# Two last differences on VectorE, later landings in the planner, and every place worked out anew in a fused attention and highway kernel

## The chip, the cores and the metric

The kernel runs on one core of a Trainium2 chip. The metric is the time of one execution on the device, in microseconds. Five engines of the core run side by side, each through its own instructions in order: TensorE (PE, with its weight loads as PEld), VectorE (DVE), ScalarE (ACT), GpSimd (POOL) and SyncE (SP). Transfers are carried by 16 DMA engines; the load queue is filled by GpSimd instructions, the store queue by SyncE, and one store by ScalarE.

## The reference

Four batches of q, k and v, each 6336 x 256 in f32. A 256 x 256 attention between channels is applied to v; the result goes row by row through a highway layer.

```python
qn = q / (np.linalg.norm(q, axis=1, keepdims=True) + 1e-06)
kn = k / (np.linalg.norm(k, axis=1, keepdims=True) + 1e-06)
s = kn.transpose(0, 2, 1) @ qn / tau
a = softmax(s)                       # over the last axis
x = (v @ a)                          # all batches: 25344 rows of 256
H = np.maximum(x @ w_h, 0.0)
T = 1.0 / (1.0 + np.exp(-(x @ w_t + b_t)))
return T * H + (1.0 - T) * x
```

## The kernel before

**Tiling.** A batch's 6336 rows are 49 slices of 128 rows and a remainder of 64. Loads bring groups of slices (QG for q and k, VG for v) and cast them to f16; q, k and v have rings of 4, 4 and 3 group buffers. A load is a GpSimd instruction, and it waits until the group that last used its buffer has been read.

**Scores.** For each slice S(b, j), TensorE adds k^T q into a 256 x 256 sum (L205, two matmuls of 256 columns) and the Gram matrix of k (L208, two of 128 columns), whose diagonal gives the norms of k. The norms of q come in one of two ways: two more matmuls of 128 columns (L214), or, for a run of four slices, squares on ScalarE (L398), a sum of halves on GpSimd (L404) and a reduction on VectorE (L411), after which the four slices need no L214. `decide` starts a run where a group has four slices left from a multiple of four and fewer than SQ_LATE runs are under way.

**The chain.** When a batch's scores are complete, `make_chain` works a chain of short steps: norms (junk, L449), square roots (ScalarE for batch 0, the GpSimd power L475 for the others), inverses and the diagonal dcat (L494, VectorE), cq on TensorE (L503), logits (L508), exponentials on ScalarE with a table load on either side (L519, L435), the normalised matrix mr (L533), its transposition at (L544), the copies at_sb (L555), the product ah with both weight matrices (L563), and its copies (L574). Then mr holds three 256 x 256 matrices, one for x, one for H and one for the gate.

**Slots.** The output is made in 100 slots of two slices (25 for each batch, the last of each with the remainder, called the odd pair). Slot t transposes v (T, L236, TensorE into PSUM), copies it to SBUF (C, L250, VectorE or ScalarE), and multiplies it by mr three times: Z into zbank, H into h, X into x (L260, four matmuls of 256 columns each). ScalarE takes the sigmoid tt of Z (L301) and seeds the bank anew with the bias (L304). VectorE makes th = max(h, 0) tt (L309) and ux = (tt - 1) x (L317). The output th - ux is a subtraction (L335) on GpSimd, except that the last DVE_SUBS slots have theirs on VectorE. Four slots make one store; the last four slots are stored singly, the very last from ScalarE's queue. LASTS puts the odd pair of the last batch at place 20 of 25.

**The order.** No scheduler of the compiler places anything. The program itself steps through a simulated time: each piece of work is a `Task` with an assumed length and a list of what it comes after, and each engine has a function (`step_pe`, `step_act`, `step_dve`, `step_pool`, `step_sp`) that picks, at each instant, the next task of its lists that is ready. The order in which tasks were picked is the order of the instructions on that engine, fixed for good; on the chip each instruction waits for what it needs. A load is assumed to land when a modelled queue has moved it, and a task that needs it may start 0.15 us later. `slot_of_score` gives the slot at which a score slice is due (from S_END), and scores of the next batch may be taken up to four slots early when TensorE has nothing else. The list `order` sorts the loads by due place. Scores of batch b + 1 are made during the slots of batch b, batch 0's scores alone at the start. A store is held while the DMA queues are full unless ORING - 3 groups of output are ready.

Of instruction names in the text: S, T, C, Z, H, X with a number are those tasks of a slice or slot, k1.0 is group 0 of batch 1 of k.

Of the kernel before, what the change touches and what calls it, by code (L numbers as in the profile page):

```python
# [60 lines left out]
def kernel(  # L61
# [13 lines left out]
    B, N, C = q.shape  # L75
# [4 lines left out]
    NS = N // P  # L80
# [3 lines left out]
    NPAIR = (NS + 1) // 2  # L84
    NSLOT = B * NPAIR
# [7 lines left out]
        return got  # L93

    QG = [spans(4, 8, 8, 8, 8, 8, 3, 2), spans(4, 4, 12, 12, 12, 5)]
    QG += [spans(4, 12, 12, 12, 9)] * (B - 2)
    VG = [spans(8, 8, 8, 12, 13)] + [spans(12, 12, 12, 13)] * (B - 1)
    GT = {"q": 12, "k": 12, "v": 13}
    CH = 4
    SQR, SQ_LATE = 4, 2  # L100
    CLOSE = 44
    DVE_SUBS, ACT_COPIES = 1, 77
    QRING, VRING, ORING = 4, 3, 7
    TTR, THR, VTR = 4, 4, 6
    OG = 4
    LASTS = list(range(20)) + [NPAIR - 1] + list(range(20, NPAIR - 1))
    PAIRS = [list(range(NPAIR))] * (B - 1) + [LASTS]
    S_END = [18, 43, 68]

    ctx.enter_context(tc.manual_schedule())  # L110
    const_pool = ctx.enter_context(tc.tile_pool(name="consts", bufs=1))
# [21 lines left out]
    MM = lambda n: n / 2400.0 + 0.0025  # L133
    PE_LAG, LAG, TO_PE = 0.20, 0.08, 0.10
    TILE = 0.309
    STEP = 0.01

# [244 lines left out]
    def make_run(b, g, j):  # L384
        n = len(runs)
        first = n == 0 or runs[-1].name[1] != b
        half = 1 if first else 2

        def area(m):
            if m % SQR == len(areas):  # L390
                areas.append(
                    work_pool.tile([P, CH + 1, C], f32, tag=f"sq{m}", bufs=1, name=f"sq{m}")
                )
            return areas[m % SQR]

        def square(e):
            o = j - QG[b][g][0]
            nc.scalar.activation(  # L398
                out=area(n)[:, 1:, :], in_=tiles["q", b, g][:, o : o + CH, :], func=Act.Square
            )  # L400

        def halves(e):
            sq = area(n)
            nc.gpsimd.tensor_tensor(  # L404
                out=sq[:, 1 : 1 + half, :], in0=sq[:, 1 : 1 + half, :],
                in1=sq[:, 1 + CH - half : 1 + CH, :], op=AluOp.add,
            )

        def reduce(e):
            lo = 1 if first else 0  # L410
            nc.vector.tensor_reduce(  # L411
                out=area(n + 1)[:, 0, :],
                in_=area(n)[:, lo : 1 + CH - half, :].rearrange("p s c -> p c s"),
                axis=mybir.AxisListType.X, op=AluOp.add,
            )

        sq = Task(("sq", b, j), "ACT", 0.2 + CH * C / 1200.0, square)
        ad = Task(("add", b, j), "POOL", 0.1 + half * C * 0.00235, halves, [(sq, LAG)])
        rd = Task(("red", b, j), "DVE", 1.0, reduce, [(ad, LAG)])
        sq.after.append((task_of_load["q", b, g], 0.15))  # L420
        if n >= SQR:
            sq.after.append((runs[n - SQR], LAG))
        if n >= 1:
            rd.after.append((runs[n - 1], LAG))
        runs.append(rd)
        if ("q", b, g) in recycler:
            recycler["q", b, g].after.append((sq, LAG + 0.2))
        queues["ACT.sq"].append(sq)
        queues["POOL.add"].append(ad)
        queues["DVE.red"].append(rd)  # L430
# [203 lines left out]
    for g in range(len(QG[0])):  # L634
        order += [(-100 + g, "q", 0, g), (-100 + g, "k", 0, g)]
    order += [(-94.5, "remq", 0, 0), (-94.5, "remk", 0, 0)]
    order += [(-80, "q", 1, 0), (-80, "k", 1, 0), (-79, "q", 1, 1), (-79, "k", 1, 1)]
    order += [(-78, "w", 0, 0), (-78, "w", 0, 1)]
    order += [(-70, "v", 0, 0), (-69, "remv", 0, 0), (2, "remq", 0, 1), (2, "remk", 0, 1)]

# [4 lines left out]
    for b in range(1, B):  # L645
        for g in range(len(QG[b])):
            if b == 1 and g < 2:
                continue
            at = slot_of_score(b, QG[b][g][0]) - 1.0
            order += [(at, "q", b, g), (at, "k", b, g)]  # L650
    for b in range(B):
        for g in range(len(VG[b])):
            if (b, g) == (0, 0):
                continue
            order.append((b * NPAIR + VG[b][g][0] // 2 - 4, "v", b, g))
    order.sort(key=lambda x: x[0])


# [106 lines left out]
    for kind, e in (("q", "DVE"), ("k", "ACT")):  # L765
        d = Task((kind, 0, 0), "DMA", 0, None)
        task_of_load[kind, 0, 0] = d
        d.end = 6.2


    chains = {}
# [49 lines left out]
    for at, kind, b, g in order:  # L821
        if kind.startswith("rem"):
            units = (2.5 if kind == "remv" else (0.7, 1.8)[g])
            add_load((kind, 0, g), units, lambda e, kk=kind[3:], g=g: load_rem(kk, g))
            continue
        if kind == "w":
            add_load((kind, 0, g), 2.0, lambda e, g=g: load_w(g))
            for ic in range(2):
                chains[0]["ah", ic].after.append((task_of_load[kind, 0, g], 0.15))
            continue  # L830
        if (b, g) == (0, 0) and kind != "v":
            continue
        after = []
        ring = groups[kind]
        size = VRING if kind == "v" else QRING
        if len(ring) >= size:
            pb, pg = ring[-size]
            gs = (VG if kind == "v" else QG)[pb]
            lastj = gs[pg][0] + gs[pg][1] - 1
            if kind == "v":  # L840
                after.append((TR[slot_of[pb, lastj // 2]], PE_LAG + 0.2))
            else:
                after.append((score[pb, lastj], PE_LAG + 0.2))
        ring.append((b, g))
        gs = (VG if kind == "v" else QG)[b]
        add_load((kind, b, g), gs[g][1], lambda e, a=(kind, b, g): load(*a), after)
        if len(ring) > size:
            recycler[(kind,) + ring[-size - 1]] = loads[-1][0]

    for b in range(B):  # L850
        for j in range(NS + 1):
            for kind in "qk":
                d = task_of_load["rem" + kind, 0, min(b, 1)] if j == NS else \
                    task_of_load[kind, b, group_of(QG[b], j)]
                score[b, j].after.append((d, 0.15))
        for i in range(NPAIR):
            for u in range(2):
                s = 2 * i + u
                d = task_of_load["remv", 0, 0] if s == NS else \
                    task_of_load["v", b, group_of(VG[b], s)]  # L860
                TR[slot_of[b, i]].after.append((d, 0.15))

# [27 lines left out]
    def take(n, engine, now, length=None):  # L892
        task = head(n)
        if not can(task, now):
            return False
        if n == "PE.S":
            decide(*task.name[1:], now)
            if task.name[1:] in squares:
                task.length -= 2 * MM(P)
        ptr[n] += 1  # L900
        run(task, engine, now, length)
        return True

    def soon(engine, now, length):
        task = head(engine + ".chain")
        if task is None or task.name[1] not in (0, B - 1):
            return False
        if any(t.end is None for t, _ in task.after):
            return False
        return max(t.end + lag for t, lag in task.after) < now + length  # L910

    slot_now = lambda: ptr["PE.out"] // 3
    PACE = [0.0]

    def step_pe(now):
        if take("PE.chain", "PE", now):
            return True
        t = slot_now()
        s = head("PE.S")
        look = ptr["PE.T"] - t  # L920
        if s is not None:
            _, b, j = s.name
            if b == 0 or slot_of_score(b, j) <= t:
                if take("PE.S", "PE", now):
                    return True
        if look < (2 if t < NSLOT - 6 else 3) and take("PE.T", "PE", now):
            return True
        if take("PE.out", "PE", now):
            return True
        if take("PE.T", "PE", now):  # L930
            return True
        if s is not None and s.name[1] > 0:
            if slot_of_score(*s.name[1:]) <= t + 4 and take("PE.S", "PE", now):
                return True
        return False

    def step_act(now):
        for n in ("ACT.chain", "ACT.tt", "ACT.seed"):
            if take(n, "ACT", now):
                return True  # L940
        ahead = 3 if slot_now() >= ACT_COPIES and ptr["copy"] % 2 == 0 else 1
        wait = slot_now() == 0 and soon("ACT", now, 0.58)
        if not wait and ptr["copy"] - slot_now() < ahead and take("copy", "ACT", now, 0.58):
            return True
# [2 lines left out]
    def step_dve(now):  # L947
        if take("DVE.chain", "DVE", now):
            return True
        if slot_now() == 0 and soon("DVE", now, 0.42):  # L950
            return False
        ahead = 1 if slot_now() >= ACT_COPIES and ptr["copy"] % 2 == 0 else 3
        if ptr["copy"] - slot_now() < ahead and take("copy", "DVE", now, 0.42):
            return True
        if take("DVE.thux", "DVE", now) or take("DVE.sub", "DVE", now):
# [30 lines left out]
    def step_sp(now):  # L986
# [8 lines left out]
        late = nload[0] == len(loads)  # L995
        if dma.backlog(1) > 6.0:
            return False
        if dma.backlog(0) + dma.backlog(1) > 3.0 and ready_groups < ORING - 3 and not late:
            return False
        behind = None  # L1000
        if now > s.since + 0.5 and not late:
# [13 lines left out]
    free["ACT"] = free["DVE"] = 6.2  # L1015
    cast_first("q", "DVE")
    cast_first("k", "ACT")
    dma.push(1, Task("first", "DMA", 0, None), 2 * FIRST * TILE, 2.3)
    setup_done = [False, False]
    idle_dma = 0.0  # L1020
    total = len(loads) + len(store_tasks) + sum(len(x) for x in queues.values())
# [61 lines left out]
```

## Time and profile before

| | us |
|---|---|
| median of 3 runs | 278.22 |
| lowest, highest | 277.82, 280.0 |
| the profiled execution | 278.45 |
| its span, first to last instruction | 276.7 |

The mean clock granted to TensorE is 0.984 of full speed. The DMA lines of the page:

| queue | packets | MB | share of 16 engines |
|---|---|---|---|
| q0, loads issued by GpSimd | 10464 | 38.67 | 70.6% |
| q1, stores and first loads | 4786 | 26.22 | 23.9% |

Groups by busy time: the GpSimd subtraction L335 has 95 of 128 x 512 at 1290 ns; tt 100 at 596; seeds 98 at 590; th 96 at 686; ux 96 at 678; copies C 84 on VectorE at 419 and 12 on ScalarE at 579; squares 26 at 1054; halves 23 at 1272; reductions 26 at 1028. Instructions of one engine overlap a little, so two th are 0.60 to 0.61 us apart.

Landings are the start of the issuing instruction plus the time that the profile gives to landing. Some of them, in us: k1.0 37.1, q1.1 39.2, k1.1 40.4, v0.0 44.9, rem_v 45.5, q1.2 49.2, k1.2 53.0 (first read at 54.0), v0.1 55.4, k1.3 66.3 (read at 66.7), k1.4 77.3 (read at 77.9). Later loads of k land 1.8 to 9.8 us before they are read.

Rows of a timeline read: start, duration, engine, line, operation, result and operands, number of instructions merged, and in brackets how long the engine had stood idle and what ended it.

### The profile page before, as it was taken

What the parts mean: (1) busy time and instruction counts of PE and PEld (TensorE: products, weight loads), DVE (VectorE), ACT (ScalarE), POOL (GpSimd) and SP (SyncE); (2) the same over time, 40 slices, a digit from 0 to 9 for tenths busy, and PEclk for the clock granted to TensorE, in tenths of its full rate; (3) what the DMA queues carried; (4) which work ended last, traced back from release to release, by engine and by line L of the source; (5) the groups of instructions that cost most, each with busy time, mean ns of one, the idle gap of its engine ahead of it and who ended that gap; (6) DMA issues with size and microseconds to landing.
All of it is one profiled execution on the core that took longest, in us unless ns stands there. A gap on an engine that the chain in (4) does not pass through costs nothing.

```text
span 276.7 us, 6628 instructions
## 1 busy us (share of the span) xinstructions
PE 252.1 (91%) x2648; PEld 218.8 (79%) x2648; DVE 205.9 (74%) x422; ACT 174.4 (63%) x288; POOL 200.5 (72%) x211
## 2 busy tenths in 40 slices
PE   0997886999999989999999999999999979999980
PEld 0696773898989877799999887899999858999770
DVE  2000035759879799899988999899897998998891
ACT  3310035867476658867785487777764887999850
POOL 5133183599889856799999838896996568988870
PEclk9999998999999999999999999999999999999995
DMA  7999999999999999999999999999999989783352
GB/s 213 213 214 213 205 165 213 208 218 216 214 210 217 241 273 276 226 294 306 276 263 223 263 243 286 224 297 308 280 265 255 349 247 351 136 317 155 152 221 111
DMA packets 15567, 66.08 MB, mean 239 GB/s; under 512 B 1713, under 2 KB 4274, under 8 KB 12594
## 3 DMA queue, kind: packets, MB, share of 16 engines
q0 software_dynamic: 10464, 38.67, 70.6%
q1 hardware_dynamic: 4786, 26.22, 23.9%
q10 hardware_dynamic: 288, 0.79, 0.7%
q8 instruction: 20, 0.33, 0.4%
q14 instruction: 9, 0.07, 0.1%
HBM read 78.38 MB, written 25.95 MB: 377 GB/s over the span
## 4 chain that ended last, share of the span: by engine, by line
PE 73%; DVE 11%; DMA 9%; ACT 2%; issue 2%; POOL 1%; DVEq 0%
PE x L260 14%; PE zbank L260 13%; PE h L260 13%; PE S L205 13%; PE vtps L236 7%; PE G L208 6%; DMA k<-in_k_dram 5%; DMA v<-in_v_dram 3%; DVE th L309 2%; PE G L214 2%; DVE ux L317 2%; DVE vts L250 2%; DMA qk<-in_k_dram 2%; PE ah L563 2%; DVE dcat L494 1%
## 5 line engine op out<-in xcount | busy, mean ns | idle before, releaser
L335 POOL TENSOR_TENSOR o<-th,ux 128x512 f32<-128x512 f32 x95 | 121.6, 1290 | 35.2 <-DVE ux L317 31.9
L260 PEld LDWEIGHTS <-vts 128*128 128x128 f16 x1200 | 112.0, 98 | 18.3 <-issue 4.7
L205 PE MATMUL S<-q,k 128*128 128x256 f16 x392 | 81.9, 278 | 10.6 <-ACT k L763 6.6
L301 ACT ACTIVATE tt<-zbank 128x512 f32<-128x512 f32 x100 | 59.5, 596 | 48.1 <-PE zbank L260 29.8
L309 DVE SCALAR_TENSOR_TENSOR th<-h,tt 128x512 f32<-128x512 f32 (+1 forms) x104 | 68.8, 665 | 12.5 <-ACT tt L301 5.7
L208 PE MATMUL G<-k 128*128 128x128 f16 x392 | 73.9, 222 | 0.0
L317 DVE SCALAR_TENSOR_TENSOR ux<-tt,x 128x512 f32<-128x512 f32 (+1 forms) x104 | 68.0, 657 | 1.2 <-PE x L260 1.2
L260 PE MATMUL zbank<-mr,vts 128*128 128x256 f16 (+1 forms) x400 | 61.1, 274 | 0.1
L260 PE MATMUL h<-mr,vts 128*128 128x256 f16 (+1 forms) x400 | 60.9, 274 | 0.0
L260 PE MATMUL x<-mr,vts 128*128 128x256 f16 (+1 forms) x400 | 60.5, 273 | 0.4 <-DVE th L309 0.2
L304 ACT COPY zbank<-btb 128x512 f32<-128x512 f32 x98 | 57.8, 590 | 3.0
L205 PEld LDWEIGHTS <-k 128*128 128x128 f16 x392 | 39.1, 100 | 15.6 <-ACT k L763 6.6
L250 DVE COPY vts<-vtps 128x512 f16<-128x512 f16 x84 | 35.2, 419 | 8.4 <-PE vtps L236 7.3
L236 PE MATMUL vtps<-ident,v 128*128 128x128 f16 x392 | 38.5, 220 | 2.1 <-DMA v<-in_v_dram 1.1
L208 PEld LDWEIGHTS <-k 128*128 128x128 f16 x392 | 39.1, 100 | 1.1 <-issue 0.3
L236 PEld LDWEIGHTS <-v 128*128 128x128 f16 x392 | 28.1, 98 | 6.3 <-issue 2.8
L404 POOL TENSOR_TENSOR sq<-sq 128x512 f32<-128x512 f32 (+1 forms) x26 | 31.4, 1209 | 1.7 <-ACT sq L398 1.6
L155 POOL DMA_DIRECT2D q<-in_q_dram x23 | 12.9, 561 | 25.2 <-PE G L214 21.7
L449 DVE SCALAR_TENSOR_TENSOR junk<-G,ident 128x128 f32<-128x128 f32 x16 | 4.7, 291 | 31.8 <-PE G L214 31.4
L411 DVE TENSOR_REDUCE sq<-sq 128x256 f32<-128x768 f32 x26 | 26.7, 1028 | 0.9 <-POOL sq L404 0.9
L398 ACT ACTIVATE sq<-q 128x1024 f32<-128x1024 f16 x26 | 27.1, 1054 | 0.0
L214 PE MATMUL G<-q 128*128 128x128 f16 x184 | 26.3, 226 | 0.0
(67 smaller groups left out, 142.4 us busy)
## 6 DMA issues: line engine op xcount, KB each, us to landing
out_dram<-o SPq DMA_DIRECT2D x23, 1024.0 KB, 10.0
v<-in_v_dram POOLq DMA_DIRECT2D x10, 768.0 KB, 20.1
q<-in_q_dram POOLq DMA_DIRECT2D x9, 768.0 KB, 19.3
k<-in_k_dram POOLq DMA_DIRECT2D x9, 768.0 KB, 21.8
v<-in_v_dram POOLq DMA_DIRECT2D x4, 832.0 KB, 20.7
q<-in_q_dram POOLq DMA_DIRECT2D x5, 512.0 KB, 11.1
k<-in_k_dram POOLq DMA_DIRECT2D x5, 512.0 KB, 13.0
v<-in_v_dram POOLq DMA_DIRECT2D x3, 512.0 KB, 15.6
```

What stands on the lines that cost most here:

```text
L205: nc.tensor.matmul(S[:, c, :], kc, qq[0:nr, :], start=first and c == 0, stop=last and c == 1)
L208: nc.tensor.matmul(G[:, c, :], kc, kc, start=first and c == 0, stop=False, skip_group_check=True,)
L214: nc.tensor.matmul(G[:, 2 + c, :], qc, qc, start=False, stop=last and c == 1, skip_group_check=True)
L236: nc.tensor.transpose(ps[:, u, c, 0:r], vt[0:r, bass.ts(c, P)], ident[0:r, 0:r])
L250: cp(out=sb, in_=ps)
L260: nc.tensor.matmul(dst[0:r, u, :], vT_t[t][:, u, kt, 0:r], mr[:, kt, off : off + C], start=(not seeded and kt == 0 and (u == 0 or i == NPA ...
L301: nc.scalar.activation(out=tts[t], in_=zbank[t % 2], func=Act.Sigmoid)
L304: nc.scalar.copy(out=zbank[t % 2], in_=btb)
L309: nc.vector.scalar_tensor_tensor(out=ths[t][pr, us, :], in0=hx["h", t][pr, us, :], scalar=0.0, in1=tts[t][pr, us, :], op0=AluOp.max, op1=A ...
L317: nc.vector.scalar_tensor_tensor(out=uxs[t][pr, us, :], in0=tts[t][pr, us, :], scalar=1.0, in1=hx["x", t][pr, us, :], op0=AluOp.subtract, ...
L335: ins = sub.tensor_tensor(out=ot[pr, o0 + us.start : o0 + us.stop, :], in0=ths[t][pr, us, :], in1=uxs[t][pr, us, :], op=AluOp.subtract,)
L404: nc.gpsimd.tensor_tensor(out=sq[:, 1 : 1 + half, :], in0=sq[:, 1 : 1 + half, :], in1=sq[:, 1 + CH - half : 1 + CH, :], op=AluOp.add,)
```

## The change

Several numbers and rules of the planner are changed, and every instruction's place follows from it; what each instruction does is as before.

- Landing: a task may use a load LAND = 0.9 us after its modelled landing (0.15 before), and the first transfer's modelled start is 3.5 instead of 2.3.
- Loads: q1.1 and k1.1 go behind the weights, v0.0 and rem_v. v0.0 has 4 slices, v0.1 8, v0.2 12. q and k of later batches are due 3 slots ahead (1 before), v 5 (4 before). Batches 2 and 3 have q and k in six groups (4, 8, 12, 12, 8, 5) instead of five.
- TensorE, while the first chain runs, leaves alone a task whose load isn't 1.4 us past its modelled landing. Scores may be early by 2 slots instead of 4; S_END is one slot later.
- Squares: up to three runs may be under way (2 before).
- The last two subtractions are on VectorE (one before); the odd pair of the last batch is at place 16.
- Copies: while the last chain is under way (`by_act`), ScalarE takes copies early and VectorE late; the last two copies go to ScalarE.
- A store is held until ORING - 2 groups are ready.

```diff
-    QG += [spans(4, 12, 12, 12, 9)] * (B - 2)
-    VG = [spans(8, 8, 8, 12, 13)] + [spans(12, 12, 12, 13)] * (B - 1)
+    QG += [spans(4, 8, 12, 12, 8, 5)] * (B - 2)
+    VG = [spans(4, 8, 12, 12, 13)] + [spans(12, 12, 12, 13)] * (B - 1)
...
-    SQR, SQ_LATE = 4, 2
+    SQR, SQ_LATE = 4, 3
...
-    DVE_SUBS, ACT_COPIES = 1, 77
+    DVE_SUBS, ACT_COPIES = 2, 77
...
-    LASTS = list(range(20)) + [NPAIR - 1] + list(range(20, NPAIR - 1))
+    LASTS = list(range(16)) + [NPAIR - 1] + list(range(16, NPAIR - 1))
...
-    S_END = [18, 43, 68]
+    S_END = [19, 44, 69]
...
-    STEP = 0.01
+    STEP, LAND = 0.01, 0.9
...
-        sq.after.append((task_of_load["q", b, g], 0.15))
+        sq.after.append((task_of_load["q", b, g], LAND))
...
-    order += [(-80, "q", 1, 0), (-80, "k", 1, 0), (-79, "q", 1, 1), (-79, "k", 1, 1)]
+    order += [(-80, "q", 1, 0), (-80, "k", 1, 0), (-65, "q", 1, 1), (-65, "k", 1, 1)]
...
-            at = slot_of_score(b, QG[b][g][0]) - 1.0
+            at = slot_of_score(b, QG[b][g][0]) - 3.0
...
-            order.append((b * NPAIR + VG[b][g][0] // 2 - 4, "v", b, g))
+            order.append((b * NPAIR + VG[b][g][0] // 2 - 5, "v", b, g))
...
-        d.end = 6.2
+        d.end = 6.25 - LAND
...
-                chains[0]["ah", ic].after.append((task_of_load[kind, 0, g], 0.15))
+                chains[0]["ah", ic].after.append((task_of_load[kind, 0, g], LAND))
...
-                score[b, j].after.append((d, 0.15))
+                score[b, j].after.append((d, LAND))
...
-                TR[slot_of[b, i]].after.append((d, 0.15))
+                TR[slot_of[b, i]].after.append((d, LAND))
...
+        if engine == "PE" and slot_now() == 0 and score[0, NS].end is not None:
+            if any(t.engine == "DMA" and t.end + LAND + 0.5 > now for t, _ in task.after):
+                return False
...
+    def by_act():
+        c = chains[B - 1]
+        return c["nq"].end is not None and c["ahc", 1].end is None
...
-            if slot_of_score(*s.name[1:]) <= t + 4 and take("PE.S", "PE", now):
+            if slot_of_score(*s.name[1:]) <= t + 2 and take("PE.S", "PE", now):
...
-        ahead = 3 if slot_now() >= ACT_COPIES and ptr["copy"] % 2 == 0 else 1
+        ahead = 3 if by_act() or slot_now() >= ACT_COPIES and (ptr["copy"] % 2 == 0 or ptr["copy"] >= NSLOT - 2) else 1
...
-        ahead = 1 if slot_now() >= ACT_COPIES and ptr["copy"] % 2 == 0 else 3
+        ahead = 1 if by_act() or slot_now() >= ACT_COPIES and (ptr["copy"] % 2 == 0 or ptr["copy"] >= NSLOT - 2) else 3
...
-        if dma.backlog(0) + dma.backlog(1) > 3.0 and ready_groups < ORING - 3 and not late:
+        if dma.backlog(0) + dma.backlog(1) > 3.0 and ready_groups < ORING - 2 and not late:
...
-    dma.push(1, Task("first", "DMA", 0, None), 2 * FIRST * TILE, 2.3)
+    dma.push(1, Task("first", "DMA", 0, None), 2 * FIRST * TILE, 3.5)
```

## The prediction

> **What bounds the kernel now.** I read the engine shares and the 40 slices first, then a table of windows, then the timeline where a window had a hole, then landing and first use of every load.
>
> ```profile
> PE 252.1 (91%) x2648; PEld 218.8 (79%) x2648; DVE 205.9 (74%) x422; ACT 174.4 (63%) x288; POOL 200.5 (72%) x211
> ```
>
> TensorE has by far the most work. From the table of windows (length, then PE, PEld, DVE, ACT, POOL busy, clock, DMA share, GB/s):
>
> ```profile
> 40.00:45.00 5.00, 2.33 (x22) 1.72 (x22) 2.11 (x8) 1.73 (x6) 2.27 (x4) 1.00 1.22 206
> 45.00:50.00 5.00, 4.85 (x32) 3.01 (x33) 2.02 (x4) 3.63 (x6) 1.08 (x2) 0.66 1.05 218
> 120.00:130.00 10.00, 10.00 (x112) 9.18 (x111) 9.55 (x16) 7.76 (x12) 9.62 (x10) 1.00 1.03 296
> 220.00:230.00 10.00, 8.55 (x73) 5.86 (x72) 9.14 (x21) 8.31 (x16) 7.43 (x7) 1.00 0.91 261
> ```
>
> Between the softmax chains TensorE has no hole (10.00 of 10), with VectorE, GpSimd and the DMA engines (1.03) close behind. Only fewer matmuls or fewer holes help, and the holes are at the chains: the first (40 to 50 us, where the clock also falls), the second (90 to 110) and the last (220 to 230). I count a hole as the distance between successive matmul starts minus 0.109 us per 256-column matmul and 0.055 per 128-column one, the steady spacing in this timeline (four of 256 take 0.44). That gives about 5.4 us from 39 to 50 us, 2.6 from 90 to 110, 0.6 from 150 to 160 and 2.9 from 220 to 230. TensorE's part of the timeline in the first chain:
>
> ```profile
> 40.43 0.28 PE L205 MATMUL S<-q,k 128*128 128x256 f16 x1 [0.99 <-DMA k<-in_k_dram]
> ...
> 41.10 0.65 PE L503 MATMUL cq<-dcat,taus 128*128 128x256 f32 x2
> ...
> 43.55 0.28 PE L544 MATMUL at<-ident,mr 128*128 128x128 f16 x2 [1.14 <-DVE mr L533]
> 44.93 0.40 PE L236 MATMUL vtps<-ident,v 128*128 128x128 f16 x4 [1.10 <-DMA v<-in_v_dram]
> 45.16 0.28 PE L544 MATMUL at<-ident,mr 128*128 128x128 f16 x2
> 45.28 1.66 PE L563 MATMUL ah<-wht,at_sb 128*128 128x512 f16 x4
> ```
>
> Twice the chain stands behind something that needs a load. cq, whose dcat was done at 39.69, starts at 41.10 because score tiles of k1.1 (landed 40.4) are ahead of it; the second at, ready at 43.98, starts at 45.16 behind a transposition of v0.0 (landed 44.9).
>
> **The first chain: about -1.2 us.** The new plan issues k1.0, then both halves of wht, v0.0 (4 slices instead of 8) and rem_v, and only then q1.1, k1.1. The loads moved ahead need no buffer of a score group, so the GpSimd queue no longer holds them until 35.1, where q1.1 waits for group 5. In the trace q1.0 and k1.0 land at 35.9 and 37.1 and q1.1 only at 39.2: 2.1 us for four slices that otherwise take about 1.2 (the eight of v0.0 took 2.4), so 0.85 us of DMA is regained. Chained at the trace's pace: wht about 39.2, v0.0 40.4, rem_v 41.1, q1.1 42.3, k1.1 43.5. TensorE now runs S1.0 to S1.3, cq, T0, T1, at, at, S1.4, ah, ah, S1.5 to S1.7, Z0. cq starts at 39.75 rather than 41.10, so both at come by 42.7. But S1.4 is in front of ah and waits for k1.1 until 43.55, and the clock will again have dropped:
>
> ```profile
> 46.00:47.00 1.00, 1.00 (x5) 0.50 1.07 221
> ```
>
> The next two slices of 1 us show 0.50 too, and 49 to 50 shows 0.94: half clock for some 3.3 us after steady work resumes. From 43.55 the new order has 2.2 us of work before Z0 (S1.4 0.33, ah 0.88, three tiles 1.0); at half clock until about 47 this ends near 47.2, where Z0 started before (47.16), but Z0, H0 and X0 then run at full speed: 1.3 us instead of 2.45. The Trainium skill's "TensorE: Matmul & The Clock Gate" (Part 1: The HAM clock gate) asks about 3.4 us without work before the clock drops, in a free-running window; by its words this shorter, interrupted hole might keep full clock, and the sum would be -2.4. The row (a drop after 42.2 to 45.2, a broken hole too) decides for -1.2.
>
> What is late next: k1.2 has v0.1 ahead of it now, four slices more: 53.0 + 1.24 - 0.85 = 53.4. TensorE gets to S1.8 at 48.5 (end of X0) + 9 x 0.44 + 4 x 0.22 + 0.3 for VectorE = 53.6. It just fits. In this stage k1.3 and k1.4 landed only 0.4 and 0.5 us before use; in the new order the same amount precedes them, so they land about 0.85 earlier. T2 needs v0.1 (about 46) at 48.5.
>
> **Two more runs of squares: -0.9 us.** The instruction order has 28 runs of squares instead of 26: 16 q-Gram matmuls fewer, x 0.055. In exchange ACT gets two squares (1.05 each), GpSimd two additions (1.27), VectorE two reductions (1.03). The smaller q/k groups also add two groups, four more DMA issues on GpSimd (0.56 each). Their cover is the idle time of those engines from 110 to 210 us: GpSimd is busy 86.5 of 100 there, so 4.7 us more find 13.5. If that cover is gone they cost up to 4.7.
>
> **The chains of batches 1 and 2: -1.1 and 0.** In the second chain cq waited 1.02 us because the two dcat took 1.81 us, beside two GpSimd operations (rows of the timeline on both engines):
>
> ```profile
> 98.28 1.28 POOL L335 TENSOR_TENSOR o<-th,ux 128x512 f32<-128x512 f32 x1
> ...
> 98.51 1.81 DVE L494 TENSOR_SCALAR dcat<-ident,inv 128x128 f32<-128x128 f32 x2
> ...
> 99.52 0.72 POOL L404 TENSOR_TENSOR sq<-sq 128x256 f32<-128x256 f32 x1
> ```
>
> In the first chain, with GpSimd idle, the same two took 0.48. Now one subtraction and no addition follows the roots on GpSimd, so one block of up to 1.28 remains. TensorE has 5.0 us queued between the last score and cq (3 T, 7 of Z/H/X, 3 S), and even the blocked dcat is ready after some 4.2. I leave 0.5 of the 1.6 us hole at cq and at. In the third chain (holes 0.6) the new order is alike: 0, between -0.6 and +0.6.
>
> **The last chain: -0.7.** Before, TensorE ran dry at T73/T74 and the two at: holes of 0.96, 0.28, 0.34, 0.49 and some smaller, 11.3 us from the last score to the end of ah for 8.8 us of work. Now 9.4 us of work is placed there, Z72 to X73 ahead of at, and ScalarE takes two copies (0.58 each) off VectorE. By the rows VectorE gives the second mr about 9.3 us after the scores (th, ux, copy, th, ux in front, 0.6 each) and ScalarE frees its seed at about 11.2 after its 4.2 us of exponentials and table loads. I get 1.2 of hole until ah and 0.55 before Z74: 1.75 for about 2.5. Bounds: 0 and -2.
>
> **The tail: +0.7.**
>
> ```profile
> 267.53 2.55 POOL L335 TENSOR_TENSOR o<-th,ux 128x512 f32<-128x512 f32 x2 [0.61 <-DVE ux L317]
> ...
> 269.21 0.68 DVE L317 SCALAR_TENSOR_TENSOR ux<-tt,x 128x512 f32<-128x512 f32 x1
> 269.92 0.70 DVE L335 TENSOR_TENSOR o<-th,ux 128x512 f32<-128x512 f32 x1
> 270.65 0.35 ACTq L352 DMA_DIRECT2D out_dram<-o  x1
> ```
>
> The end hangs on VectorE's last subtraction, then a store of 2.1 us. Now two subtractions follow the last ux on VectorE. The last copy moves to ScalarE (VectorE -0.33), but stands there before the second-last sigmoid, so th98 starts at 267.46 instead of 267.37; 0.1 + 0.6 = 0.7. The Trainium skill ("SBUF — State Buffer", SBUF: two separate sides) speaks against the change here: a VectorE operation with two SBUF inputs shares a locked port with GpSimd, so an overlap could add one GpSimd subtraction, 1.28. But GpSimd's last is now sub97, over by 268.8, and the first moved one starts at 270.0; I take the row.
>
> The odd pair of the last batch, four slots earlier, keeps its extra 0.65 us: 0. Stores may wait for one more ready group; their cover is the DMA share of 0.48 and 0.45 after 250 us: 0 here.
>
> **Sum.** -1.2 - 0.9 - 1.1 + 0 - 0.7 + 0.7 = -3.2 from the profiled execution's 278.45 (span 276.7 and 1.75 around it) gives 275.3. That execution is 0.2 above the median of 278.22.
>
> **The rivals.** (1) The gain is eaten on the way, about 278.5. Batch 1 is fed by landings until 86 us (margins 0.4 to 1.0), so if the 0.85 us of DMA isn't regained, k1.2 lands at 54.2 and the first chain gives -0.5; if dcat and mr are blocked again and the last chain stays dry, only the squares and the tail are left: -0.5 - 0.9 + 0.7 = -0.7, up to 280 if a chain gets worse. For: fixed orders met other durations in all four chains. Against: each of the named waits has lost its visible cause. (2) Slower, about 282.7: GpSimd becomes the bound in batches 2 and 3. It is at 9.6 to 9.8 of 10 from 120 to 150, and the added 4.7 us then come in full, with the squares and chains 1 and 3 worth nothing: -1.2 + 4.7 + 0.7. It decides once its idle time from 110 to 210 shrinks to what the chains force on it, about 5 us. Against: VectorE waits for a GpSimd result before th there only once (0.70 us at 196). (3) The edits do little, since the front of the DMA queue is bandwidth either way: inside (1).
>
> **How the numbers follow.** The forecast (273 to 277) gets 0.58, rival 1 (277 to 280) 0.27, rival 2 (281 to 284) 0.15. The range 273.0 to 281.0 leaves out rival 2 and a little below. This measurement can tell about 1% from no change: faster means under 275.4, slower over 281.0. Three quarters of the forecast lie under 275.4: 0.43; rival 2 gives slower, with a little of rival 1: 0.16; the rest, 0.41, is within 1%. The likeliest case's own range is 273.5 to 277.
>
> **What would show it.** Right: cq near 39.8, the first ah before 44.5, no wait for v in the first chain; no wait of 0.5 us for k before S1.8; holes under 1 us from 90 to 110 and under 2 from 220 to 230; 168 q-Gram matmuls of 128 columns instead of 184; two VectorE subtractions at the end, the last ending 3.1 us after the last group of matmuls starts (268.24), against 2.4 now. Wrong: TensorE waits for k or v of 1 us or more between 47 and 90, GpSimd over 9.8 of 10 throughout with VectorE waiting for o, or the clock below 1 in a second place.

## The result and the profile after

| us | before | after |
|---|---|---|
| median of 4 runs each, beside each other | 278.48 | 274.85 |
| lowest, highest | 277.82, 280.0 | 274.61, 275.68 |
| the profiled execution | 278.45 | 274.83 |
| its span, first to last instruction | 276.7 | 272.7 |
| mean clock granted to TensorE | 0.984 | 0.995 |

The changed kernel takes 0.987 of the time before (95% interval 0.982 to 0.991), 3.6 us less. The forecast was 275.3 with a range of 273.0 to 281.0, so the total came out within half a microsecond. Its parts did not all come out; that is what the rest is about.

First the engine shares of the kernel after, then its table of windows (columns as before: length, then PE, PEld, DVE, ACT, POOL busy with counts, clock, DMA share, GB/s).

```profile
PE 248.5 (91%) x2632; PEld 216.5 (79%) x2632; DVE 207.3 (76%) x423; ACT 176.4 (65%) x292; POOL 204.3 (75%) x216
```

```profile
40.00:45.00 5.00, 3.60 (x32) 2.42 (x33) 3.36 (x11) 3.17 (x9) 2.50 (x4) 1.00 1.13 222
45.00:50.00 5.00, 4.98 (x53) 4.42 (x51) 3.18 (x8) 4.65 (x9) 2.26 (x3) 1.00 1.03 213
120.00:130.00 10.00, 10.00 (x113) 9.17 (x111) 9.39 (x17) 7.93 (x12) 9.29 (x10) 1.00 1.04 299
220.00:230.00 10.00, 8.34 (x69) 5.67 (x70) 9.49 (x23) 7.64 (x16) 6.15 (x7) 1.00 1.03 312
```

The reader is to see four things. TensorE has 16 matmuls fewer (2632). In the first chain it does more in the same 10 us (85 records instead of 54), and the clock stayed at 1.00 where it was 0.66. From 120 to 130 nothing changed: TensorE is full, and GpSimd is at 9.29, not at its end. And the last chain, 220 to 230, did not become fuller: 8.34 busy instead of 8.55.

The first chain on TensorE, from the timeline after:

```profile
39.92 0.67 PE L503 MATMUL cq<-dcat,taus 128*128 128x256 f32 x2 [0.41 <-DVE nrm L484]
40.42 0.39 PE L236 MATMUL vtps<-ident,v 128*128 128x128 f16 x4
41.76 0.38 PE L236 MATMUL vtps<-ident,v 128*128 128x128 f16 x4 [0.95 <-DVE vts L250]
42.38 0.28 PE L544 MATMUL at<-ident,mr 128*128 128x128 f16 x2 [0.23 <-DVE mr L533]
42.88 0.28 PE L544 MATMUL at<-ident,mr 128*128 128x128 f16 x2 [0.21 <-DVE mr L533]
43.35 1.03 PE L563 MATMUL ah<-wht,at_sb 128*128 128x512 f16 x4
45.21 0.60 PE L260 MATMUL zbank<-mr,vts 128*128 128x256 f16 x4
...
52.80 0.28 PE L205 MATMUL S<-q,k 128*128 128x256 f16 x1 [0.63 <-DMA k<-in_k_dram]
```

No wait for k or v is left before 46 us: cq starts at 39.92 instead of 41.10, ah at 43.35 instead of 45.28. The last line shows where the gain meets its limit: S1.8 waits for k1.2, which landed at 52.8.

Where the 3.6 us came from can be added up. I count lost time on TensorE much as in the prediction: the start of a milestone less the matmul work ahead of it at 0.109 us per 256 columns and 0.056 per 128, an f32 matmul at twice that (its own spacing in the traces, 0.216 and 0.112).

| lost on TensorE in the stretch, us | before | after | difference |
|---|---|---|---|
| start to S1.49 (first chain, batch 1 fed by landings) | 22.11 | 20.70 | -1.41 |
| S1.49 to Z25 (second chain) | 2.74 | 2.09 | -0.65 |
| Z25 to S2.49 | 0.13 | 0.19 | +0.06 |
| S2.49 to Z50 (third chain) | 1.58 | 1.61 | +0.03 |
| Z50 to S3.49 | 0.37 | 0.15 | -0.22 |
| S3.49 to Z75 (last chain) | 3.26 | 3.61 | +0.35 |
| Z75 to X99 | 0.94 | 0.95 | +0.01 |
| sum | 31.13 | 29.30 | -1.83 |

To that come -0.89 for the 16 matmuls less, by their spacing (X99 starts at 265.52 instead of 268.24, which is -1.83 - 0.89), +0.52 from X99 to the end of VectorE's last subtraction, -1.80 from there to the end of the span, and +0.38 outside the span (2.13 instead of 1.75 between span and time). That makes -3.62.

The tail after, VectorE and the last store:

```profile
266.54 0.68 DVE L317 SCALAR_TENSOR_TENSOR ux<-tt,x 128x512 f32<-128x512 f32 x1
267.13 1.29 DVE L335 TENSOR_TENSOR o<-th,ux 128x512 f32<-128x512 f32 x2
268.45 0.35 ACTq L352 DMA_DIRECT2D out_dram<-o  x1
```

Two subtractions now stand at the end, and the last ends at 268.42, 2.90 us behind the start of X99 (2.38 before). The span ends at 272.7, which is 4.28 us later; before it was 6.08. The last store is not what ends it: it lands 2.1 us after its issue in both, at 270.5 and before at 272.8. What ends last is GpSimd's closing DRAIN, an instruction at the last line of the program, which the timeline does not list. The view of that line (engine, operation, number; shortest, median and longest in ns; first and last start in us) has before:

```profile
L1078 POOLq DRAIN  x3: 45/102/7153, 268.7 to 276.4; - x3
```

After:

```profile
L1085 POOLq DRAIN  x3: 45/93/7470, 264.4 to 272.4; - x3
```

The long one is the first of the three. It is issued as GpSimd's last subtraction starts and ends at 275.9 before and 271.9 after, with 0.8 us of closing steps behind it in both. GpSimd's last subtraction after:

```profile
264.46 1.30 POOL L335 TENSOR_TENSOR o<-th,ux 128x512 f32<-128x512 f32 x1 [0.16 <-DVE ux L317]
```

It ends at 265.76, 0.24 us behind the start of X99. Before, it ended at 270.08, 1.84 behind. The DRAIN ends 5.8 us behind that subtraction before, and 6.1 after. So with the second-last subtraction on VectorE, GpSimd is done 1.60 us nearer to X99, the DRAIN takes 0.32 more behind it, and the end of the span comes 1.28 us nearer (+0.52 - 1.80), though the last result comes later. SyncE's closing wait, which a view puts down to TensorE's queue, ends with the DRAIN and shrank with it (longest 3.0 us before, 1.3 after).

So nearly half of the gain lies behind the last result, in a place that the prediction had no term for. The cause is read from the traces; no run moved that subtraction alone, and what the DRAIN itself waits for is not shown. By the same times SyncE has seen the store land by 270.8, 1.1 us ahead of the DRAIN's end. A third subtraction on VectorE would put about 0.6 on that side (the pace of the two above), so an estimate of what it could still bring is half a microsecond.

### The profile page after: what moved, and what is told of

Its sections match the earlier page's. It is cut to its first block, busy times and chain, and to the rows that moved or that the text cites. A ratio compares the mean times of both kernels' runs of the same rounds, so it can differ in the third digit from the quotient of the medians.

```text
span 272.7 us, 6603 instructions
## 1 busy us (share of the span) xinstructions
PE 248.5 (91%) x2632; PEld 216.5 (79%) x2632; DVE 207.3 (76%) x423; ACT 176.4 (65%) x292; POOL 204.3 (75%) x216
## 4 chain that ended last, share of the span: by engine, by line
PE 73%; DMA 13%; DVE 9%; issue 1%; POOL 1%; ACT 0%; DVEq 0%
PE zbank L260 14%; PE x L260 14%; PE h L260 14%; PE S L205 13%; DMA k<-in_k_dram 11%; PE vtps L236 7%; PE G L208 6%; PE G L214 2%; DVE th L309 2%; DMA qk<-in_k_dram 2%; DVE ux L317 2%; DVE mr L533 1%; DVE vts L250 1%; DVE nrm L484 1%; PE ah L563 1%
## 5 line engine op out<-in xcount | busy, mean ns | idle before, releaser
L260 PEld LDWEIGHTS <-vts 128*128 128x128 f16 (+1 forms) x1200 | 111.2, 98 | 18.4 <-issue 6.4
L205 PE MATMUL S<-q,k 128*128 128x256 f16 x392 | 80.7, 276 | 12.1 <-ACT k L763 6.3
L208 PE MATMUL G<-k 128*128 128x128 f16 x392 | 73.1, 221 | 0.0
L250 DVE COPY vts<-vtps 128x512 f16<-128x512 f16 x82 | 34.4, 420 | 6.3 <-PE vtps L236 5.3
L404 POOL TENSOR_TENSOR sq<-sq 128x512 f32<-128x512 f32 (+1 forms) x28 | 33.9, 1211 | 3.2 <-ACT sq L398 3.2
L155 POOL DMA_DIRECT2D q<-in_q_dram x25 | 14.1, 564 | 22.7 <-PE G L214 20.3
L411 DVE TENSOR_REDUCE sq<-sq 128x256 f32<-128x768 f32 x28 | 28.8, 1029 | 1.8 <-POOL sq L404 1.8
L398 ACT ACTIVATE sq<-q 128x1024 f32<-128x1024 f16 x28 | 29.2, 1053 | 0.0
L214 PE MATMUL G<-q 128*128 128x128 f16 x168 | 23.7, 224 | 0.0
```

Source lines behind the costliest of these rows:

```text
L205: nc.tensor.matmul(S[:, c, :], kc, qq[0:nr, :], start=first and c == 0, stop=last and c == 1)
L208: nc.tensor.matmul(G[:, c, :], kc, kc, start=first and c == 0, stop=False, skip_group_check=True,)
L250: cp(out=sb, in_=ps)
L260: nc.tensor.matmul(dst[0:r, u, :], vT_t[t][:, u, kt, 0:r], mr[:, kt, off : off + C], start=(not seeded and kt == 0 and (u == 0 or i == NPA ...
L398: nc.scalar.activation(out=area(n)[:, 1:, :], in_=tiles["q", b, g][:, o : o + CH, :], func=Act.Square)
L404: nc.gpsimd.tensor_tensor(out=sq[:, 1 : 1 + half, :], in0=sq[:, 1 : 1 + half, :], in1=sq[:, 1 + CH - half : 1 + CH, :], op=AluOp.add,)
```

## The experiments

Four kernels ran on one chip, beside 23 runs of the kernel before (median 278.66, 277.9 to 280.33).

| kernel | median us | lowest, highest | runs | ratio to before, interval | profiled | clock |
|---|---|---|---|---|---|---|
| e0_after | 274.55 | 274.46, 274.66 | 4 | 0.983 (0.980 to 0.985) | 274.66 | 0.985 |
| e1_hole | 279.25 | 276.78, 279.98 | 12 | 0.999 (0.996 to 1.002) | 279.0 | 0.978 |
| e2_loads | 279.89 | 279.53, 281.96 | 12 | 1.005 (1.002 to 1.007) | 279.79 | 0.997 |
| e6_mr | 274.2 | 273.84, 274.98 | 5 | 0.982 (0.979 to 0.984) | 274.98 | 0.982 |

**e0_after: the changed kernel once more.** No edit. It asks what of the first profile comes again: the kept clock, and the shorter end.

> The changed kernel once more, beside which the other three of this call are read. Both theories: 0.985 to 0.989 of the kernel before. A look at the end: theory A, the 1.8 us less between the last subtraction's end and the end of the span (4.25 after, 6.05 before) belongs to one execution and not to the change, so this profile may show anything from 4 to 6; theory B, the change shortens the end, and it is 4.2 again.

The time came again (274.66, 274.83 in the first profile), but the clock did not. TensorE's windows (length, busy, clock, DMA share, GB/s) of the first profile of the changed kernel (40 to 50 us are shown further up, at 1.00):

```profile
50.00:55.00 5.00, 4.10 (x45) 1.00 1.00 206
60.00:65.00 5.00, 4.39 (x46) 1.00 1.04 217
```

and of e0_after:

```profile
40.00:45.00 5.00, 3.61 (x22) 0.77 1.11 219
45.00:50.00 5.00, 5.00 (x49) 0.89 1.04 216
50.00:55.00 5.00, 4.72 (x51) 1.00 1.01 206
60.00:65.00 5.00, 4.99 (x56) 1.00 1.05 217
```

With the same order of instructions and the same landings, the clock fell here at about 42.7 us, and Z0 started at 46.70 instead of 45.21. But at Z8 the two executions are level again (63.60 and 63.67). The other rows say how: the execution with the full clock waits 0.63 us for k1.2 and 0.87 for two th between 50 and 66, and the one with the fallen clock only 0.27, for one th. The 1.5 us are absorbed by waits that come later. The end behind the last subtraction is 4.2 us again, as theory B had it, so it is a property of the kernel and not of one execution. All four kernels of this table have the last two subtractions on VectorE and an end of 4.2 to 4.3, with the DRAIN ending 6.1 us behind GpSimd's last subtraction.

**e1_hole: a longer first chain.** Two more activation table loads on ScalarE make the first exponentials 2.5 us later than in e0_after (43.52 to 41.01); the order of everything else is the same.

```diff
-            add("table", "ACT", 1.5, lambda e: preload_table(Act.Exp), [(T["root", "k"], 0.0)])
+            add("table", "ACT", 1.5, lambda e: [preload_table(f) for f in (Act.Exp, Act.Sqrt, Act.Exp)],
+                [(T["root", "k"], 0.0)])
```

> The changed kernel, the order of all work the same, but two table loads with their one-column activations more on ScalarE in the first chain (1.28 + 0.20 us each, 3 us in all), so the exponentials start about 2.4 us later and TensorE has a longer hole before its first slot. Theory A (the clock makes half of the first chain's gain, and loads give half of it back): the clock falls to 0.5 for about 3 us after the hole, X0 comes 2.4 + 1 us or more later, but TensorE then waits less for k1.2 (0.63 us before S1.8 now), so by the end of batch 1's scores only some 1.5 to 2.5 us are left: ratio to the changed kernel 1.006 to 1.009. Theory B (no clock, no give-back): clock stays 1.00, the end is 2.4 us later, 1.009, and the k1.2 wait is as long as now.

TensorE's timeline of e1_hole:

```profile
41.70 0.38 PE L236 MATMUL vtps<-ident,v 128*128 128x128 f16 x4 [0.95 <-DVE vts L250]
44.75 0.89 PE L544 MATMUL at<-ident,mr 128*128 128x128 f16 x4 [2.67 <-DVE mr L533]
...
49.68 0.60 PE L260 MATMUL zbank<-mr,vts 128*128 128x256 f16 x4
```

Z0 is 2.98 us later than in e0_after (49.68 to 46.70), and nothing of it comes back: Z8 is 2.98 later, S1.49 2.97, S3.49 2.99. The clock fell, which theory B had excluded (half from 42.8 to 49.7 us by windows of 1 us), but nothing was given back, which theory A had counted on. The two results together say why: in e0_after a wait of only 0.27 us is left between 50 and 66, so the cover that took up 1.5 us of clock is used up, and what comes on top goes through in full. One can lose about 1.5 us in the first chain for nothing, and pays for the next 3 to the end.

Then the last chain loses more, though nothing was changed there. TensorE's windows of e1_hole, same columns:

```profile
45.00:50.00 5.00, 4.90 (x27) 0.53 1.05 218
...
226.00:231.00 5.00, 4.92 (x22) 0.66 1.04 267
```

From 226 to 231 the granted clock was 0.66 (1.00 in e0_after, with 51 matmul records instead of 22). From S3.49 to Z75, 4.90 us are lost instead of 3.57. The median is 1.7% above e0_after, where the theories had 0.6 to 0.9%. The 12 runs fall apart in the same way: three with a mean clock of 0.991 or 0.992 take 276.78 to 277.89, nine with 0.972 to 0.979 take 279.0 to 279.98. The half clock in the last chain is the likely difference; only one execution has a trace, so for the others it is read from the mean clock alone.

**e2_loads: the load order undone.** q1.1 and k1.1 go back to their due places; all else of the change stays.

```diff
-    order += [(-80, "q", 1, 0), (-80, "k", 1, 0), (-65, "q", 1, 1), (-65, "k", 1, 1)]
+    order += [(-80, "q", 1, 0), (-80, "k", 1, 0), (-79, "q", 1, 1), (-79, "k", 1, 1)]
```

> The changed kernel with q1.1 and k1.1 loaded ahead of the weights and v0.0 again; the planner orders the rest for it. Theory A (the order of loads makes the first chain's gain): cq or a transposition waits for a load again, X0 is 1.5 us or more later than 46.1, the clock falls, and the time is 0.3 to 0.6% above the changed kernel. Theory B (the later assumed landing and the rule that TensorE leaves loads alone are enough, whatever the order): X0 within 0.7 us, the time within 0.2%.

It is 5.3 us slower than e0_after (1.9%, more than either theory had), but not in the first chain. X0 starts at 46.51, within 0.5 us of the first profile of the changed kernel (46.08), as theory B had it, though k1.2 now lands late enough for S1.8 to wait 1.32 us (54.30), and at S1.49 only 0.41 us more is lost than in that profile (21.11 to 20.70). The rest comes later, against the same profile: 1.99 us more from S1.49 to Z25, and 2.49 more from S2.49 to Z50. Because the planner steps through its own time, one moved load gives every engine another order, and the other chains meet other neighbours. VectorE's timeline of e2_loads in the second chain:

```profile
104.67 0.15 DVE L530 RECIPROCAL rinv<-rs 128x1 f32<-128x1 f32 x1
104.86 2.54 DVE L533 TENSOR_SCALAR mr<-ssb,rinv 128x256 f16<-128x256 f32 x1
```

and GpSimd's at the same time:

```profile
104.28 0.61 POOL L155 DMA_DIRECT2D v<-in_v_dram  x1
104.89 0.54 POOL L155 DMA_DIRECT2D q<-in_q_dram  x1
105.41 0.54 POOL L155 DMA_DIRECT2D k<-in_k_dram  x1
105.97 1.28 POOL L335 TENSOR_TENSOR o<-th,ux 128x512 f32<-128x512 f32 x1
```

An operation of 0.35 us was held until 107.40, just after the subtraction ended (107.25), and TensorE's at waited 1.46 us for it. So as an undoing of one part this run failed: it changed the plan of three other chains. What it does show is that the planner's result differs by 2% for a change that its own first chain hardly feels. It puts no clean price on the load order by itself. For the first chain alone it gives an estimate: with the old order k1.2 lands 1.5 us later (54.3 to 52.8), and by S1.49 that costs 0.41.

**e6_mr: two operations of VectorE swapped.** In the last chain after, the second mr stands on VectorE behind ux71, and so meets a subtraction on GpSimd. VectorE's timeline of the changed kernel:

```profile
220.61 0.68 DVE L317 SCALAR_TENSOR_TENSOR ux<-tt,x 128x512 f32<-128x512 f32 x1
221.21 0.15 DVE L530 RECIPROCAL rinv<-rs 128x1 f32<-128x1 f32 x1
221.39 1.42 DVE L533 TENSOR_SCALAR mr<-ssb,rinv 128x256 f16<-128x256 f32 x1
```

GpSimd's:

```profile
221.38 1.28 POOL L335 TENSOR_TENSOR o<-th,ux 128x512 f32<-128x512 f32 x1 [0.30 <-DVE rinv L530]
```

and TensorE's:

```profile
221.34 0.27 PE L544 MATMUL at<-ident,mr 128*128 128x128 f16 x2
223.19 0.27 PE L544 MATMUL at<-ident,mr 128*128 128x128 f16 x2 [1.58 <-DVE at_sb L555]
```

The subtraction that blocks mr is the one that ux71 itself let go. (The bracket names rinv; the subtraction reads ux, which was done just before.) The Trainium skill, "SBUF — State Buffer" (SBUF: two separate sides), describes a port pair that VectorE and GpSimd share under a lock held for the whole instruction; the 1.42 us beside a 1.28 us subtraction agree. The edit puts the second mr in front of ux71 and touches no other place:

```diff
+    soft, late = chains[B - 1]["softmax", 1], UX[71]
+    mr_late, ux_late = soft.emit, late.emit
+    late.emit = lambda e: (mr_late(e), ux_late(e))[1]
+    soft.emit = None
```

> The changed kernel, but in the last chain the second inverse and mr are issued on VectorE ahead of ux71 instead of behind it; nothing else moves. Theory A (the 1.42 us of that mr is GpSimd's subtraction, released by ux71 and holding what both engines need): mr takes 0.35 to 0.5, at follows by 221.7, ah ends 1 to 1.8 us earlier, the time falls by 0.6 to 1.2 us (0.2 to 0.45%). Theory B (the last chain is bound by ScalarE, whose table loads and seeds hold Z74 anyway): mr gets short, Z74 starts at 224.9 as now, and the time stays within 0.1%.

VectorE's timeline of e6_mr:

```profile
220.89 0.49 DVE L533 TENSOR_SCALAR mr<-ssb,rinv 128x256 f16<-128x256 f32 x1
221.31 0.15 DVE L530 RECIPROCAL rinv<-rs 128x1 f32<-128x1 f32 x1
221.49 0.37 DVE L533 TENSOR_SCALAR mr<-ssb,rinv 128x256 f16<-128x256 f32 x1
221.79 0.67 DVE L317 SCALAR_TENSOR_TENSOR ux<-tt,x 128x512 f32<-128x512 f32 x1
```

TensorE's:

```profile
222.51 0.27 PE L544 MATMUL at<-ident,mr 128*128 128x128 f16 x2 [0.42 <-DVE ux L317]
223.30 0.27 PE L544 MATMUL at<-ident,mr 128*128 128x128 f16 x2 [0.52 <-DVE at_sb L555]
```

The blocked operation is gone (0.37 instead of 1.42) and the wait before the second at fell from 1.58 to 0.52, but the first at, at 221.34 before without a wait, now waits 0.42, and the trace names ux71 as what lets it go. (In the changed kernel it also started just after ux71's end, at 221.29.) From S3.49 to Z75, 3.01 us are lost instead of 3.57 in e0_after: 0.56 of the 1.06 that went from the second wait. That is between the two theories. The median fell by 0.35 us (274.2 to 274.55), less than the intervals of the two ratios can part. The profiled execution of e6_mr was its slowest, at half clock twice, in batch 0's scores and in the first chain. TensorE's windows of e6_mr:

```profile
28.00:29.00 1.00, 1.00 (x10) 0.50 0.99 201
...
45.00:50.00 5.00, 5.00 (x38) 0.70 1.06 218
```

Only the first of the two is new against e0_after. The loads came later too (q1.0 issued at 31.81 instead of 30.14, k1.2 landed at 53.4 instead of 52.7), and 21.00 us are lost by Z8 (20.22 in e0_after), long before the swap. Among runs of like mean clock, the three of e6_mr at 0.992 to 0.996 (273.84 to 274.2) lie about 0.5 below the three of e0_after at 0.994 to 0.998 (274.46 to 274.58). These are few runs and were chosen after the fact. e6_mr is the fastest version measured; that it beats the changed kernel is likely and not settled.

Not tried, and so open: one subtraction on VectorE instead of two, which would test the end of the span, squares in at most two runs, the chain without the rule for copies on ScalarE, and the new load order alone on the kernel before.

## Why the prediction was right, and where it was not

**First chain: forecast -1.2, measured -1.4 by S1.49.** The landings were worked out to within 0.6 us: v0.0 40.4 forecast and 39.9 measured, q1.1 42.3 and 41.7, k1.1 43.5 and 42.9, k1.2 53.4 and 52.8. So the 0.85 us of DMA was regained, and somewhat more. It paid less than the forecast had it: e2_loads, without it, loses only 0.41 us more by S1.49, so some 1.0 of the 1.4 seems to come from the rest of the edits (an estimate, since the plan of e2_loads differs and its clock held).

The size rested on the clock, -1.2 if it fell and -2.4 if not. In e0_after it fell, to half from 42.7 to 46.1 us by windows of 1 us, and the working is nearly met: Z0 at 46.70 for a forecast of 47.2, then full clock, and X0 at 47.58, 1.57 us earlier than before (49.15). In the first profile it held, and the kernel took the same time: by the wait for k1.2 and two waits for th, TensorE gets no more than about 1.5 us through to Z8. That cap is what -2.4 left out. The prediction had its number (k1.2 "just fits") without using it so. The rule of the Trainium skill's "TensorE: Matmul & The Clock Gate" (Part 1: The HAM clock gate) had the clock right in one execution and the row of the trace in the other. A free-running window would give both; no run here sets its place.

**Squares: forecast -0.9, by count -0.89.** 168 q-Gram matmuls, as forecast; no run takes them out alone. GpSimd stayed at 9.3 of 10 from 120 to 130 and at 90.3 of 100 from 110 to 210 (86.5 before), and TensorE had no wait of any kind listed from 150 to 176, so rival 2 did not come about.

**Second chain: forecast -1.1, measured -0.65.** The step that failed is "one block of up to 1.28 remains". dcat came free, and the wait of 1.02 us at cq went with it, but two other operations were held. VectorE's timeline after:

```profile
94.51 1.35 DVE L484 TENSOR_SCALAR nrm<-nrm 128x2 f32<-128x2 f32 x1
...
101.61 1.48 DVE L533 TENSOR_SCALAR mr<-ssb,rinv 128x256 f16<-128x256 f32 x1
```

GpSimd's after:

```profile
94.55 1.29 POOL L335 TENSOR_TENSOR o<-th,ux 128x512 f32<-128x512 f32 x1
...
100.39 2.56 POOL L335 TENSOR_TENSOR o<-th,ux 128x512 f32<-128x512 f32 x2 [1.23 <-DVE ux L317]
```

Behind the held nrm stands a copy for which a transposition then waited 0.41 us (at 97.23), and the first at waited 0.45 for the held mr (at 103.15). That of mr was no news, for VectorE's timeline before has it in this chain:

```profile
104.72 1.38 DVE L533 TENSOR_SCALAR mr<-ssb,rinv 128x256 f16<-128x256 f32 x1
```

I priced the hold at dcat only, and not at the other two operations of its kind in the same chain. An operation on two columns, 0.16 us when alone, is held as long as a large one.

**Third chain: forecast 0, measured +0.03.**

**Last chain: forecast -0.7, measured +0.35.** The same omission, and the largest error of the sum. The working had mr at the pace of th, ux and copies at 0.6 each and no place for a lock; mr took 1.42, the second at waited 1.58 for what followed, and e6_mr won 0.56 back by a swap. The bound "0 and -2" excluded a loss for no stated reason. The swap itself put a wait of 0.42 in front of the first at. Without that, the 1.06 by which the second at's wait fell is as large as the error of 1.05; no run shows the two apart.

**Tail: forecast +0.7, measured +0.52 to the last subtraction.** th98, the two subtractions and the pace were as written. The lock did not strike there, as forecast: the two took 1.29 together.

**Behind the tail: no term, measured -1.42** (-1.80 in the span, +0.38 around it). The step that failed is "The end hangs on VectorE's last subtraction, then a store of 2.1 us". It hung on GpSimd, whose DRAIN ends some 6 us behind its last subtraction, and the edit that was charged +0.7 took a subtraction off GpSimd. From X99 to the end of the span that made -1.28 instead. Without the -1.42 the sum would have been -2.2, not -3.2, since the four chains gave -1.68 for a forecast of -3.0. Two errors of opposite sign met: that the total came out so close is luck.

Rival 1 had part of the mechanism (a blocked mr, a last chain that stays dry), but gave up the first chain too, which held.

## What to carry over

A hole in front of a chain is worth no more than the distance to the next landing that TensorE will wait for; work out that cap before arguing about the clock. Where a trace shows VectorE held for the length of a GpSimd subtraction, go through every short VectorE operation of a chain, not only those that a trace shows blocked, and ask which GpSimd operation will have just been let go when it starts; putting it ahead of the operation that lets it go is a swap of two lines. In an order that a planner makes, a constant undone is a new plan, not an undone part: test by swapping two instructions in the finished order. Before pricing a tail, look at the program's last line for the engine that ends last; it need not be the one with the last result.

## What was not expected of the hardware

- The same instructions in the same order kept full clock from 40 to 50 us in one execution and got 0.77 and 0.89 of it in another. By windows of 1 us the half clock lasted 3.4 us in the kernel before and in e0_after, and 6.8 in e1_hole, and it started at 45.7, 42.7 and 42.8 us.
- GpSimd's closing DRAIN lasted 7.2 us in the kernel before and 7.5 in the five later profiles, and ended 5.8 and 6.1 us behind GpSimd's last subtraction. So an engine that was done 2.7 us before the last result (265.76 to 268.42) still ended the span.
- In e2_loads mr was held 2.54 us beside two load issues of GpSimd and a subtraction, longer than any one of them; in e6_mr it took 0.37 beside a load issue (221.18 to 221.77). Nor was GpSimd idle in the first chain before, as the prediction says: the two dcat took 0.48 there (39.21 to 39.69) beside a load issue (39.27 to 39.87). Whether issues hold the lock, and which, is open.
